# A fused attention and FFN kernel: a third pair of batches in seven products, attention in whole float32

## The chip, the core and the metric

The kernel runs on one core of one Trainium2 chip. The time is device microseconds from the first to the last instruction with what lies around them; a run's number is one execution, and the number of a kernel is the median of its runs. Five engines take part: TensorE (PE in the profile, its weight loads PEld), VectorE (DVE), ScalarE (ACT), GpSimd (POOL) and SyncE (SP), which here issues every DMA. SBUF has 128 partitions; PSUM, into which TensorE writes, has eight banks here used as 512 float32 columns each.

## The reference

Eight batches, twelve heads of 64, 448 positions, width 768, hidden width 3072:

```python
scores = q @ k.T / sqrt(64) - log(448)        # per batch and head
x = sigmoid(scores) @ v                       # 8 x 12 x 448 x 64, laid out as 8 x 448 x 768
h = (x.T @ U) @ V                             # mixing over positions, rank 32
u = x + h.T
out = u + relu(u @ w_ch1) @ w_ch2             # 768 -> 3072 -> 768
```

All arrays are float32. The launch hands U, V and both weight matrices over as 64-bit words (`np.asarray(...)` viewed as int64), and the kernel makes float32 of them itself.

## The kernel before

**Stages.** Attention of a batch goes pair of heads by pair of heads (`pair`, L583): scores of a tile of 128 keys by 448 queries for both heads (`scores_of`, L535, matmuls in L547; the last 64 keys of two neighbouring pairs share a tile, L551), a sigmoid (L664), and values (`values_of`, L557, matmuls in L566 and for the shared tile in L576). Two neighbouring pairs are here called a quad; a batch has three. The result x lies in six tiles `ua` or `ub` of 128 channels by 448 positions. `mix` (batches 0 and 1) or `mix_half` (the others, three tiles at a time, matmuls L848 and L858) adds the mixing over positions; the sum u is written to DRAM (`parked`) for all batches but 0.

**Half precision in parts.** Most matmuls take an fp16 high part and an fp16 rest of each operand and add three products (high by high, high by rest, rest by high). The helper `rest` (L404) makes the rest on VectorE, `scaled` (L401) the high part on GpSimd. `decode` (L874) makes such parts of the weights: 48 pieces of 768 KB are loaded (`w_in`), turned into float32 on VectorE (L404) and ScalarE (L453), bounded (L464), split and kept in DRAM (`kept`). In attention the batches 0 and 1 (`WHOLE = 2`) use whole float32 matmuls; for the batches 2 to 7 q, k and v are scaled and split, and each sigmoid tile is copied to fp16 (L692, ScalarE) and its rest made (L404, VectorE).

**The FFN.** The first `PLAIN = 4` batches go one by one: per batch 24 chains of 18 matmuls into the hidden layer (`ffn_in`, L938) and 36 chains of 12 out of it (`ffn_out`, L958), 864 matmuls. The last four batches go in two pairs by a scheme of seven products in place of eight on 2 x 2 blocks (Strassen's scheme in Winograd's form): `in_quad` and `out_quad`, 12 calls each of 63 matmuls, all in L1146. It needs sums of weight blocks (`quarter_sums`: GpSimd L998 and L1002, then ScalarE L1009 and VectorE L1010, kept as `forms`) and sums of the two batches' u (`far_forms`, `near_forms` for the first pair, `u_forms` for the next).

**What sets the order.** The class `Plan` collects every operation with an engine, a cost, what it reads and writes, the buffers that it wants and a place `pos`. `Plan.order` then builds one program per engine: again and again it takes, where something can start first, the operation with the lowest place. `BOND` keeps TensorE at one kind of attention matmul, `LATE` is the slack that it gives to TensorE's operations after their inputs (0.546 before). The constants at the head (L59 to L74) place the stages against each other: `BEGIN` gives the begin of each batch's FFN, `LATER` the order of the batches 2 to 7 in attention. What this prints is a fixed order for each engine; on the chip an engine waits for its next instruction's inputs and never takes a later one first.

**Homes.** Buffers that are not in use at the same time lie in the same SBUF: the decoding's float32 pieces (`T32`) lie over `stg` (the split q, k, v), over `at` (sigmoids before splitting) and over the second of two `us` (u in fp16 parts for the plain FFN); the mixing's `xs` and `xt` lie in `w64`, in which the weights arrive. `qk` has three homes, `v` four, `a` (sigmoids) seven.

Of the kernel before, what the change touches and what calls it, by code (L numbers as in the profile page):

```python
# [61 lines left out]
ROOM0, ROOM, AHEAD, BEFORE, PACE = -7.852, 308.311, -53.442, 95.466, 1.111  # L62
PREP, BOUNDS, VALUES, SECOND, MIXED = 19.918, -15.21, 0.731, 3.0, 3.524
MIXED1, MIX_1 = 6.837, -10.814
MIX_2, EV_IN, EV_OUT, A_OFF = 34.703, 70.659, 39.745, -7.081
START, DECODE = 63.04, 64.674
U_AT, U_STEP = -3.425, 6.242
LEAD, SUMS, STEP_K, STEP_I, FFN_LEAD = -5.194, 216.012, 10.066, 62.433, 60.97
W_AT, W_STEP, PAIR0, MIX0A, MIX0B, W2_LAG, G0_LEAD = -69.485, 11.668, 3.029, -290.85, -260.87, 0.576, -7.653
LOW_G = 1  # L70
FB, AB = 8, 0
# [23 lines left out]
class Plan:  # L95
# [37 lines left out]
    def order(self):  # L133
# [19 lines left out]
        def room(i):  # L153

            when, taken = 0.0, []
            for t in self.ops[i][7]:
                if t.got is None:
                    if t.in_turn and self.queues[t.name][0] is not t:
                        return None
# [75 lines left out]
def fused_kernel(ctx: ExitStack, tc: tile.TileContext, q, k, v, wu, wv, w1, w2, out):  # L235
# [29 lines left out]
    US = ring("us", 2, [NP, 2, S], F16)  # L265
# [4 lines left out]
    a_, at_ = buf("a", [14 * S], F32), buf("at", [4 * S], F32)  # L270
    A2 = [Buffer(a_[:, 2 * i * S : 2 * (i + 1) * S]) for i in range(7)]
    AT2 = [Buffer(at_[:, 2 * i * S : 2 * (i + 1) * S]) for i in range(2)]
    QK = ring("qk", 3, [2, S], F32)
    V32 = ring("v", 4, [4, P], F32)
# [11 lines left out]
    for x in XT + XS:  # L286
        x.shares += WSRC
        WSRC[0].shares.append(x)
    for x in XT + XS + WS + WSRC:
        x.shares += W64  # L290
        for b in W64:
            b.shares.append(x)
# [55 lines left out]
    for i in range(8):  # L348
        spots(stg[:, 2 * i * S : 2 * (i + 1) * S], under(2 * i * S, 2 * (i + 1) * S))
# [1060 lines left out]
```

## Time and profile before

| What | Value |
|---|---|
| Median of 3 runs | 1537.73 us (1536.45 to 1542.45) |
| The profiled execution | 1541.77 us, of it 1540.0 us from the first to the last instruction |
| Granted TensorE clock, mean | 0.996 |
| Moved by DMA | 306.01 MB |

A page of the profile gives each engine's busy time, a chain of work followed back from the last instruction, and groups of instructions by line. The windows view gives the same busy times for stretches of the span: length, then for PE, PEld, DVE, ACT and POOL the busy us and in brackets the number of instructions, then the granted TensorE clock, the busy share of the DMA engines and GB/s. A row of the chain has start, length and what ran; of the timeline, start, length, engine, line, operation, names and shape. A float32 matmul stands as two records in the chain and in the timeline.

### The profile page before, as it was taken

What the parts mean: (1) busy time and instruction counts of PE and PEld (TensorE: products, weight loads), DVE (VectorE), ACT (ScalarE), POOL (GpSimd) and SP (SyncE); (2) the same over time, 40 slices, a digit from 0 to 9 for tenths busy, and PEclk for the clock granted to TensorE, in tenths of its full rate; (3) what the DMA queues carried; (4) which work ended last, traced back from release to release, by engine and by line L of the source; (5) the groups of instructions that cost most, each with busy time, mean ns of one, the idle gap of its engine ahead of it and who ended that gap; (6) DMA issues with size and microseconds to landing.
All of it is one profiled execution on the core that took longest, in us unless ns stands there. A gap on an engine that the chain in (4) does not pass through costs nothing.

```text
span 1540.0 us, 23899 instructions
## 1 busy us (share of the span) xinstructions
PE 1520.0 (99%) x8843; PEld 752.1 (49%) x8843; DVE 1110.4 (72%) x1864; ACT 814.6 (53%) x1327; POOL 381.9 (25%) x538
## 2 busy tenths in 40 slices
PE   8999899999999999999999999999999999999999
PEld 3344455544444444444444444555555555555554
DVE  2788898668878868766678776776867777565656
ACT  5598766478666666666587735332332614131310
POOL 0110001554234462221322540045454500000000
PEclk9899999999999999999999999999999999999999
DMA  7789876675756858555777656866665673443331
GB/s 215 248 300 272 291 260 253 247 257 162 196 156 171 248 180 208 160 158 167 224 217 205 183 213 173 266 216 229 238 233 180 219 251 113 121 126 108 108 108 72
DMA packets 184725, 306.01 MB, mean 199 GB/s; under 512 B 54560, under 2 KB 146080, under 8 KB 178464
## 3 DMA queue, kind: packets, MB, share of 16 engines
q1 hardware_dynamic: 184608, 304.49, 63.5%
q8 instruction: 69, 1.13, 0.3%
q14 instruction: 48, 0.39, 0.1%
HBM read 232.88 MB, written 63.26 MB: 192 GB/s over the span
## 4 chain that ended last, share of the span: by engine, by line
PE 91%; DMA 4%; DVE 2%; ACT 1%; issue 1%; POOL 0%; SPq 0%; ACTq 0%; POOLq 0%
PE banks L1146 37%; PE banks L958 20%; PE banks L938 19%; PE banks L547 6%; PE banks L566 5%; DMA w<-w_in 2%; PE banks L551 1%; PE banks L576 1%; PE banks L848 1%; DMA qk__99<-q_in 1%; DMA qk__99<-k_in 1%; PE banks L858 0%; DVE stg L404 0%; DMA v__104<-v_in 0%; PE banks L790 0%
## 5 line engine op out<-in xcount | busy, mean ns | idle before, releaser
L958 PE MATMUL banks<-h__94,w__92 128*128 128x448 f16 x792 | 157.9, 353 | 4.3 <-DVE xnt L404 3.2
L958 PE MATMUL banks<-h__93,w__91 128*128 128x448 f16 x792 | 157.8, 353 | 0.7 <-ACT h__94 L946 0.7
L404 DVE SCALAR_TENSOR_TENSOR a<-at,a 128x896 f16<-128x896 f32 (+1 forms) x129 | 141.3, 1118 | 14.9 <-ACT a L692 14.5
L938 PEld LDWEIGHTS <-w__90 128*128 128x128 f16 x936 | 91.1, 98 | 88.7 <-issue 5.4
L958 PEld LDWEIGHTS <-w__92 128*128 128x128 f16 x864 | 82.1, 98 | 88.0 <-issue 15.5
L958 PEld LDWEIGHTS <-w__91 128*128 128x128 f16 x864 | 82.0, 98 | 85.8 <-issue 13.0
L1146 PEld LDWEIGHTS <-w__89 128*128 128x128 f16 x819 | 80.1, 98 | 74.8
L1146 PEld LDWEIGHTS <-w__92 128*128 128x128 f16 x819 | 80.1, 98 | 74.7
L1146 PEld LDWEIGHTS <-w__90 128*128 128x128 f16 x819 | 80.1, 98 | 74.6
L692 ACT ACTIVATE a<-at 128x896 f16<-128x896 f32 x126 | 115.3, 950 | 0.6
L938 PEld LDWEIGHTS <-w__89 128*128 128x128 f16 x792 | 77.0, 98 | 74.1 <-issue 3.5
L1002 POOL TENSOR_TENSOR w<-w 128x384 f32<-128x384 f32 x96 | 105.7, 1101 | 4.8
L938 PE MATMUL banks<-us__87,w__90 128*128 128x448 f16 x504 | 99.1, 352 | 2.3 <-ACT h__94 L946 2.3
L938 PE MATMUL banks<-us__88,w__90 128*128 128x448 f16 x432 | 85.5, 353 | 0.0
L938 PE MATMUL banks<-us__88,w__89 128*128 128x448 f16 x432 | 84.8, 353 | 0.0
L1146 PEld LDWEIGHTS <-w__91 128*128 128x128 f16 x567 | 55.5, 98 | 51.8
L998 POOL TENSOR_TENSOR w<-w 128x384 f32<-128x384 f16 x48 | 44.6, 959 | 117.1 <-DVE xnt L1010 82.0
L547 PE MATMUL banks<-stg 64*128 64x448 f16 x648 | 72.7, 351 | 0.0
L938 PE MATMUL banks<-us__87,w__89 128*128 128x448 f16 x360 | 71.1, 353 | 0.0
L566 PE MATMUL banks<-a,stg 128*64 128x448 f16 x648 | 68.2, 355 | 0.0
L945 ACT ACTIVATE r__95<-banks 128x448 f32<-128x448 f32 x48 | 25.9, 539 | 74.2 <-PE banks L938 73.4
L1009 ACT CAST xnt<-w 128x1536 f16<-128x1536 f32 x24 | 35.2, 1468 | 29.4 <-POOL w L1002 29.4
(1119 smaller groups left out, 3068.4 us busy)
## 6 DMA issues: line engine op xcount, KB each, us to landing
w<-w_in SPq DMA_DIRECT2D x48, 768.0 KB, 6.8
forms<-xnt SPq DMA_DIRECT2D x24, 768.0 KB, 4.4
w__89<-kept SPq DMA_DIRECT2D x9, 1536.0 KB, 7.4
w__90<-kept SPq DMA_DIRECT2D x9, 1536.0 KB, 7.2
w__91<-kept SPq DMA_DIRECT2D x9, 1536.0 KB, 8.5
w__92<-kept SPq DMA_DIRECT2D x9, 1536.0 KB, 7.8
w__90<-forms SPq DMA_DIRECT2D x13, 768.0 KB, 5.4
w__89<-forms SPq DMA_DIRECT2D x13, 768.0 KB, 5.8
```

Source lines behind the costliest of these rows:

```text
L404: nc.vector.scalar_tensor_tensor(out=out, in0=in0, scalar=s, in1=in1, op0=op0, op1=op1)
L547: nc.tensor.matmul(sc[j].x[:, h, :S], x[rows_of(h), j * P : j * P + P], y[rows_of(h)], start=i == 0, stop=i == n - 1)
L551: nc.tensor.matmul(sc[j].x[rows_of(m), h, :S], x[rows_of(h), 3 * P : S], y[rows_of(h)], start=i == 0, stop=i == n - 1)
L566: nc.tensor.matmul(av.x[rows_of(h), :S], x[:, j, rows_of(h)], y(tiles[j], h), start=j == 0 and i == 0, stop=not quad and j == 2 and i == n ...
L692: act(0.95, lambda a=a, to=to: nc.scalar.activation(half(a, 0), to.x, AF.Copy, scale=A_UP), kto, [(a, 0)], here + A_OFF)
L938: nc.tensor.matmul(ph.x[:, :S], w.x[:, f, c, x], us.x[:, c, y, :], start=c == 0 and i == 0, stop=c == NP - 1 and i == 2,)
L945: act(0.54, lambda: nc.scalar.activation(r.x, ph.x[:, :S], AF.Relu, scale=DOWN_H), [ph], [r], pos - EV_IN)
L958: nc.tensor.matmul(po.x[:, :S], w.x[:, f, e, x], h.x[:, f, y, :], start=f == 0 and i == 0, stop=f == FC - 1 and i == 2,)
L998: pool(0.93, lambda j=j: nc.gpsimd.tensor_tensor(out=t.x[:, j], in0=quarter(j, 0), in1=quarter(j, 1), op=ALU.add), [w] if b is None else k ...
L1002: pool(1.0, lambda o_=o_, x=x, y=y, sub=sub: nc.gpsimd.tensor_tensor(out=t.x[:, o_], in0=t.x[:, x], in1=t.x[:, y], op=ALU.subtract if sub ...
L1009: act(1.45, lambda: nc.scalar.copy(made(0), t.x.rearrange(order)), [(t, j) for j in range(4)], [(o, 0)], pos)
L1146: nc.tensor.matmul(bank.x[:, :S], wt[1](k, n, x), both(f)[:, y], start=start and k == i == 0, stop=k == 2 and i == 2, skip_group_check=True)
```

## The change

Six things change together.

1. `PLAIN` goes from 4 to 2: the batches 0 and 1 go one by one, and (2, 3), (4, 5), (6, 7) in seven products. The sums of weight blocks that were spread over three plain batches are all made in batch 1.
2. Attention of all batches is in whole float32 matmuls, as that of 0 and 1 was (`SC32`, `VA32`). The scaling, splitting and bounding of q, k and v, and the splitting of the sigmoids, are not called any more. The sigmoid's output is the value matmuls' input.
3. The value banks are copied out by VectorE (`OUTD`, L751 now) and no longer by ScalarE (L703 before).
4. Homes: `xs` and `xt` get SBUF of their own (`xst`) and no longer share `w64` with the weights; the decoding's pieces lie over `stg` and a new buffer `t32`; `us` has one home in place of two; q and k of batch 0 may also lie in the halves of `h`.
5. A score block, a transpose of the mixing and the first chain into a home of `h` now also wait, in the planner, until the home that their result goes to is free (`"place"`).
6. All constants are new, among them `BOND` (6.183 to 34.831) and `LATE` (0.546 to -2.868: the planner may take an operation of TensorE up to 2.9 us before its inputs are there). Attention of the batches 2 to 7 now begins in the FFN of batch 0.

```diff
 WHOLE = 2
-PLAIN = 4
-LATER = [2, 4, 3, 5, 6, 7]
-FORMS = {1: (0,), 2: (1,), 3: (2,)}
+SC32 = (0, 1, 2, 3, 4, 5, 6, 7)
+VA32 = (0, 1, 2, 3, 4, 5, 6, 7)
+OUTD = (0, 1, 2, 3, 4, 5, 6, 7)
+PLAIN = 2
+LATER = [2, 3, 4, 5, 6, 7]
+FORMS = {1: (0, 1, 2)}
...
-SWITCH, BOND = 0.11, 6.183
-PIPE, LANDS, LATE = 0.33e6, 3.237, 0.546
+SWITCH, BOND = 0.11, 34.831
+PIPE, LANDS, LATE = 0.33e6, 3.237, -2.868
...
-    US = ring("us", 2, [NP, 2, S], F16)
+    US = ring("us", 1, [NP, 2, S], F16)
...
-        n = 1 if b < WHOLE else 3
+        n = 1 if b in SC32 else 3
...
+            if b == 0 or j % 2 == 0:
+                js = (j,) if b == 0 or j and not odd else (j, j + 1)
+                for m in js:
+                    tiles[m] = plan.tile("a2", A2)
+                places = [(tiles[m], "place") for m in js]
...
-            to = a if whole else plan.tile("t2", AT2)
+            to = a if wv else plan.tile("t2", AT2)
...
+            if b in OUTD and wv:
+                dve(0.6, lambda ku=ku, bank=bank: nc.vector.tensor_copy(ku.x, bank.x[:, :S]), [bank], [ku], late)
...
-    XT = [Buffer(w64h[:, : NP * S].rearrange("p (n d) -> p n d", d=P))]
-    XS = [Buffer(w64h[:, NP * S : 2 * NP * S].rearrange("p (c x s) -> p c x s", c=3, x=2))]
+    xst = buf("xst", [2 * NP * S], F16)
+    XT = [Buffer(xst[:, : NP * S].rearrange("p (n d) -> p n d", d=P))]
+    XS = [Buffer(xst[:, NP * S :].rearrange("p (c x s) -> p c x s", c=3, x=2))]
...
-        qk, v32 = plan.tile("qk", QK), plan.tile("v", V32)
+        qk, v32 = plan.tile("qk", QK + QH if b == 0 else QK), plan.tile("v", V32)
...
-            d = (BEGIN[PLAIN] - AHEAD - BEGIN[1]) / (NP * len(LATER) + 0.5)
+            d = (BEGIN[PLAIN] - AHEAD - BEGIN[0] - LATER_AT) / (NP * len(LATER) + 0.5)
             for j, x in enumerate(LATER):
-                attention(x, BEGIN[1] + NP * d * j, d)
+                attention(x, BEGIN[0] + LATER_AT + NP * d * j, d)
```

What this makes of the order is shown at two places. The first is SyncE at the start of the program: `qk` and `v` are homes of q, k and v, `w` the buffer in which weight words arrive, `_in` the inputs in DRAM. Before:

```order
L378 DMA qk__99<-k_in 64x448
L378 DMA qk__99<-q_in 64x448
L378 DMA qk__99<-k_in 64x448
L378 DMA qk__99<-q_in 64x448
L378 DMA v__102<-v_in 128x512
L378 DMA qk__100<-k_in 64x448
L378 DMA qk__100<-q_in 64x448
```

Now:

```order
L408 DMA w_106<-w_in 128x6x128 x2
L408 DMA qk__98<-k_in 64x448
L408 DMA qk__98<-q_in 64x448
L408 DMA qk__98<-k_in 64x448
L408 DMA qk__98<-q_in 64x448
L408 DMA v__101<-v_in 128x512
L408 DMA w_106<-w_in 128x6x128
```

Two weight loads now stand ahead of the first k and q, and a third behind the first v; before, the first three stood together behind the loads of three pairs.

The second is ScalarE in the middle of the attention stage. `a` are sigmoids, `at` sigmoids that are still to be split, `banks` PSUM, `r` and `h` the hidden layer, `ub` the attention's result, `junk` the output that nobody reads of a bound. Before:

```order
L664 ACTIVATE at<-banks,bias_s,c__211 128x896 x2
L692 ACTIVATE a<-at 128x896 x2
L664 ACTIVATE at<-banks,bias_s,c__211 128x896
L464 ACTIVATE junk,ss__194<-v__104 128x512
L692 ACTIVATE a<-at 128x896
L664 ACTIVATE at<-banks,bias_s,c__209 128x896
L464 ACTIVATE junk,ss__194<-qk__100 128x448
L692 ACTIVATE a<-at 128x896
L464 ACTIVATE junk,ss__194<-qk__100 128x448
L664 ACTIVATE at<-banks,bias_s,c__209 128x896
L945 ACTIVATE r__96<-banks 128x448
```

Now:

```order
L705 ACTIVATE a<-banks,bias_s 128x896 x2
L903 ACTIVATE xnt<-banks 128x384
L890 ACTIVATE xst<-ub__84,s_x__194 128x448
L890 ACTIVATE xst<-ub__86,s_x__194 128x448
L996 ACTIVATE r__95<-banks 128x448
L997 ACTIVATE h__94<-banks 128x448
L705 ACTIVATE a<-banks,bias_s 128x896 x5
L996 ACTIVATE r__96<-banks 128x448
L997 ACTIVATE h__94<-banks 128x448
L903 ACTIVATE xnt<-banks 128x384
L705 ACTIVATE a<-banks,bias_s 128x896 x2
```

One or two sigmoids, each followed by its copy, have become runs of up to five sigmoids without anything between, and the copies and bounds are gone.

More of the change, by code (lines that the diff above doesn't have):

```diff
@@ new lines, in fused_kernel, with laid @@
+    for j in range(stg.shape[1] // (2 * PIECE)):
+        lo, hi = j * 2 * PIECE, (j + 1) * 2 * PIECE
+        t = Buffer(stg[:, lo:hi].bitcast(F32))
+        for o in under(lo, hi):
+            t.shares.append(o)
+            o.shares.append(t)
+        T32.append(t)
+    for j in range(T32_N):
+        T32.append(Buffer(t32[:, j * PIECE : (j + 1) * PIECE]))
+        shared.append((j * PIECE, (j + 1) * PIECE, T32[-1]))
+    def laid(lo, n, ap):
+        x = Buffer(ap)
+        for a, b, o in shared:
+            if a < lo + n and lo < b:
+                x.shares.append(o)
+                o.shares.append(x)
+        return lo, lo + n, x
@@ L354, in fused_kernel @@
         spots(x.ap, [x])
+    for i in range(t32.shape[1] // S):
+        spots(t32[:, i * S : (i + 1) * S], [o for lo, hi, o in shared if lo < (i + 1) * S and i * S < hi])
     for i in range(10):
-        spots(w64[:, i * S // 2 : (i + 1) * S // 2], W64 + (WSRC if i < 4 else []) + (XT[:1] if i < 3 else []) + (XS if 3 <= i < 6 else []) + (WS if i >= 6 else []))
+        spots(w64[:, i * S // 2 : (i + 1) * S // 2], W64 + (WSRC if i < 4 else []) + (WS if i >= 6 else []))
+    FORM = SPOT[-4:] + SPOT[-10:-7]
     MID = SPOT[:-10] + SPOT[-6:-4]
+    for i in range(6):
+        spots(xst[:, 2 * i * S : 2 * (i + 1) * S], XT if i < 3 else XS)
+    MID += SPOT[-6:]
     WT = []
@@ L474, in fused_kernel @@
     for b in range(PLAIN):
-        BEGIN.append(BEGIN[-1] + FFN + (ROOM0 if not b else ROOM * len(LATER) / (PLAIN - 1)))
+        BEGIN.append(BEGIN[-1] + FFN + (ROOM0, ROOM)[b])
     def mixing():
@@ L671, in pair @@
             quads[b] = dict(last=[last_products], products=score_products, kscore=kscore, klast=klast)
[L672 to L673 removed]
+            if not ws:
+                quads[b].update(cm=cm)
+            if not wv:
+                quads[b].update(v3=v3)
             quad = None
         products = [quad["products"], score_products] if odd else [score_products]
[L676 removed]
+        sc = {}
         for j in range(3 + odd):
@@ L717, in new_u @@
     def new_u(b):
-        u32s[b] = [plan.tile(f"u{'ab'[b > 0]}{c}", [(UB if b else UA)[c]]) for c in range(NP)]
-        mxs[b] = sm("mx", NP) if b < PLAIN else sm(f"mx{b}", NP, 1)
+        u32s[b] = [plan.tile(f"u{'ab'[b > 0]}{c}", [UB[c]] if b else [UA[c]]) for c in range(NP)]
+        mxs[b] = sm(f"mx{b}", NP, 1)
     def mix(b, pos0, pos1):
@@ L754, in transposes @@
                         )
-                op_ = pe(0.48, transposes, ku[hf * 3 : hf * 3 + 3] + ["ident"] + ([] if whole else [sx]), [tr] + ([tp] if sc == 0 else []), at, after=() if sc == 0 else first)
+                xn = plan.tile("xn", XN)
+                op_ = pe(0.48, transposes, ku[hf * 3 : hf * 3 + 3] + ["ident"] + ([] if whole else [sx]), [tr, (xn, "place")] + ([tp] if sc == 0 else []), at, after=() if sc == 0 else first)
                 first = first if sc else [op_]
-                xn = plan.tile("xn", XN)
                 if whole:
@@ L933, in ffn_in @@
         ph = plan.tile("f", PF[b], False)
+        place = [(h, "place")] if f == 0 else []
         def chain():
@@ L941, in chain @@
                     )
-        entered.append(pe(18 * MM, chain, [(w, 0, f), (w, 1, f)] + [(us, c, x) for c in range(NP) for x in range(2)], [ph], pos, 0.3))
+        entered.append(pe(18 * MM, chain, [(w, 0, f), (w, 1, f)] + [(us, c, x) for c in range(NP) for x in range(2)], [ph] + place, pos, 0.3))
         r = plan.tile("r", R)
```

227 lines of the change are left out of this document (118 added, 109 removed).

## The prediction

> **What bounds the kernel now.** I read the page first, then the busy time by windows, the chain that ended last, the timeline of TensorE, and last the groups of instructions. From the page:
>
> ```profile
> span 1540.0 us, 23899 instructions
> PE 1520.0 (99%) x8843; PEld 752.1 (49%) x8843; DVE 1110.4 (72%) x1864; ACT 814.6 (53%) x1327; POOL 381.9 (25%) x538
> ```
>
> TensorE has 20 us without work; no other engine comes near. A change is worth what it does to TensorE's own work, plus what it does to those 20 us and to stretches where TensorE runs at a lower clock. Where they lie, by windows (columns: length, busy us of PE, PEld, DVE, ACT, POOL, granted clock, DMA share, GB/s):
>
> ```profile
> 0.00:40.00 40.00, 33.45 (x158) 14.36 (x159) 12.43 (x21) 22.48 (x31) 1.21 (x9) 0.96 0.75 212
> 40.00:80.00 40.00, 37.90 (x155) 13.62 (x154) 28.41 (x59) 24.91 (x39) 4.81 (x7) 0.87 0.75 247
> ...
> 160.00:200.00 40.00, 33.47 (x188) 18.42 (x187) 35.75 (x69) 30.97 (x55) 2.33 (x8) 1.00 0.83 293
> 200.00:240.00 40.00, 40.00 (x214) 20.73 (x213) 39.64 (x74) 28.25 (x49) 1.87 (x3) 1.00 0.78 274
> ...
> 480.00:560.00 80.00, 79.59 (x508) 38.38 (x506) 62.08 (x96) 54.54 (x86) 43.55 (x57) 1.00 0.77 222
> ...
> 1500.00:1540.00 40.00, 36.29 (x192) 18.59 (x190) 24.68 (x40) 3.09 (x6) 0.00 (x0) 1.00 0.19 69
> ```
>
> Idle are 6.5 us in 0 to 40, 2.1 in 40 to 80, 6.5 in 160 to 200, 3.7 at the end (the last output's drain), and about 1 in all the rest. In 160 to 240 VectorE is at 35.8 and 39.6 of 40: there it holds TensorE up, with decoding, the mixing of batch 1 and the FFN of batch 0 at once. Between 200 and 1500 TensorE hardly ever waits although VectorE works three quarters of the time.
>
> The lower clock, in 4 us windows:
>
> ```profile
> 24.00:28.00 4.00, 2.13 (x6) 1.83 (x8) 2.48 (x3) 0.71 (x3) 0.00 (x0) 0.74 0.44 122
> 28.00:32.00 4.00, 4.00 (x21) 2.05 (x19) 0.00 (x0) 3.82 (x6) 0.00 (x0) 0.83 0.86 256
> ...
> 64.00:68.00 4.00, 1.91 (x5) 0.63 (x4) 1.87 (x3) 3.57 (x6) 0.00 (x0) 0.86 0.97 328
> 68.00:72.00 4.00, 4.00 (x8) 1.44 (x6) 2.55 (x4) 1.94 (x3) 0.00 (x0) 0.50 0.53 184
> 72.00:76.00 4.00, 4.00 (x14) 1.20 (x16) 3.93 (x8) 2.46 (x3) 0.52 (x1) 0.50 0.59 197
> 76.00:80.00 4.00, 4.00 (x19) 1.48 (x17) 2.33 (x8) 4.00 (x7) 0.74 (x2) 0.86 0.54 145
> ...
> 172.00:176.00 4.00, 1.82 (x10) 0.97 (x10) 3.36 (x5) 3.46 (x7) 0.00 (x0) 1.00 0.63 256
> ```
>
> Loss by it: 4 x (0.26 + 0.17) = 1.7 us near 28, 4 x (0.14 + 0.50 + 0.50 + 0.14) = 5.1 near 70. Idle and slow clock that could go at all: 6.5 - 4.2 (the first load, below) + 2.1 + 6.5 + 1 + 6.8 = 18.7 us.
>
> **The change on TensorE's work.** Block lengths from the chain, for whole float32 (counts are records, two to a matmul), and for chains and products of the FFN:
>
> ```profile
> 4.18 7.82 PE banks L547 x23
> ...
> 25.86 4.46 PE banks L547 x12
> ...
> 80.67 0.91 PE banks L576 x8
> 81.58 0.95 PE banks L547 x4
> ...
> 82.79 1.70 PE banks L547 x8
> 84.49 2.41 PE banks L566 x12
> 86.90 3.51 PE banks L938 x18
> ...
> 91.36 0.91 PE banks L551 x8
> ...
> 126.98 3.40 PE banks L938 x18
> ...
> 1499.97 36.33 PE banks L1146 x192
> ```
>
> and for three half-precision products, from TensorE's timeline (start to the next row's start is the length):
>
> ```profile
> 577.00 1.31 PE L547 MATMUL banks<-stg 64*128 64x448 f16 x12
> 578.24 2.44 PE L958 MATMUL banks<-h__94,w__92 128*128 128x448 f16 x12
> 580.62 1.89 PE L566 MATMUL banks<-a,stg 128*64 128x448 f16 x18
> 582.44 0.76 PE L576 MATMUL banks<-a,stg 64*64 64x448 f16 x12
> 583.13 0.74 PE L547 MATMUL banks<-stg 64*128 64x448 f16 x6
> 583.81 2.44 PE L958 MATMUL banks<-h__94,w__92 128*128 128x448 f16 x12
> ```
>
> Two pairs of heads that share a last tile (I call them a quad; a batch has three) need scores of two tiles and of one, again two and one, the shared score tile, two value blocks and the shared value tile. In float32: 2 x (1.70 + 0.95) + 0.91 + 2 x 2.41 + 0.91 = 11.94 us. In three products: 2 x (1.24 + 0.68) + 0.69 + 2 x 1.82 + 0.69 = 8.86 us, taking the shared score tile like the shared value tile. Before, 6 quads are float32 and 18 are not: 231 us. After, 24 x 11.94 = 286.6. A score block pays once for its start (1.70 is two tiles and 0.95 one, so a tile is 0.75 and the start 0.20; 0.12 in half precision). Counted in the order, the 96 blocks of this sum stand as 84 runs before, 54 after: off go 42 x 0.20 = 8.4 after and about 1.8 before. Attention: 278.2 - 229.2 = **+49.0 us**.
>
> The FFN: a plain pair of batches is 2 x (24 chains of 18 + 36 of 12) = 1728 matmuls, a seven-product pair 24 x 63 = 1512. 216 matmuls less, at 36.33 / 192 = 0.189 us: **-40.9**. A plain chain just ahead of attention takes 0.1 longer (3.51 against 3.40); the order has 66 such places before and 39 after: **-2.7**. Mixing and scaling keep their matmuls. Sum of TensorE's work: **+5.4 us**.
>
> [...]
>
> **The other engines.** For 18 quads these two passes go, 126 of each, and with them the splits of q, k and v and their scales; the copies of the value banks (48) move from ScalarE to VectorE. Rows of the page:
>
> ```profile
> L404 DVE SCALAR_TENSOR_TENSOR a<-at,a 128x896 f16<-128x896 f32 (+1 forms) x129 | 141.3, 1118 | 14.9 <-ACT a L692 14.5
> ...
> L692 ACT ACTIVATE a<-at 128x896 f16<-128x896 f32 x126 | 115.3, 950 | 0.6
> L664 ACT ACTIVATE a<-banks,bias_s 128x896 f32<-128x896 f32 x42 | 40.4, 1007 | 5.5 <-PE banks L547 3.6 <-PE banks L551 1.8
> ...
> L945 ACT ACTIVATE r__95<-banks 128x448 f32<-128x448 f32 x48 | 25.9, 539 | 74.2 <-PE banks L938 73.4 <-DVE h__94 L947 0.8
> ...
> w<-w_in SPq DMA_DIRECT2D x48, 768.0 KB, 6.8
> ```
>
> These 257 us of work ran beside a full TensorE, so taking them away gives nothing by itself. They matter only where TensorE waits.
>
> **The waits, one by one.**
> 1. The first load. SyncE's order now puts two weight loads of 768 KB ahead of the first k and q, whose scores start at 4.18. An issue of such a load takes SyncE 2.06 / 3 = 0.7 us:
>
> ```profile
> 11.64 2.06 SPq L378 DMA_DIRECT2D w<-w_in  x3
> ```
>
> If only the issues count it is 1.4 us; if the two are served first, the second is issued at 1.4 and landed 6.8 later, and q follows after its own 1.4 us of further issues: 9.6, so 5.4. Nothing covers it. Nearer to the second: **+4**.
> 2. The wait near 24 (2.4 idle, 1.7 of clock): three weight loads issued at once stood between the pairs of batch 0 and k and q had three homes. Now the weight loads stand singly and the last three pairs land in the homes of h. Gone: **-4.1**; at the other end it stays, 0.
> 3. 64 to 80 (2.1 idle, 5.1 of clock): mixing of batch 0 in float32 waits for ScalarE and VectorE, both busy with decoding. In the order 11 pairs' value blocks stand ahead of the first FFN chain where 9 stood, so there is more to put between, but mixing and decoding still meet: half, **-3.6**, between 0 and -7.2.
> 4. 160 to 200 (6.5): VectorE full. Between the first and the last output chain of batch 0 there now stand 15 pairs of attention, where 2 stood; at some 6 us a pair TensorE gives the same decoding 78 us more, and decoding and mixing no longer share w64. **-6**, between 0 and -6.5.
> 5. New: runs of scores. The order has 15 runs of five float32 tiles. TensorE needs 5 x 0.75 + 0.20 = 3.95 us, ScalarE's sigmoids 5 x 1.007 = 5.04, and the eight banks hold four tiles. The value block that follows reads its first three tiles first, which gives ScalarE time. **+2**; at worst the difference, 15 x 1.1 = 16.5, and twice that with a pair of relus (2 x 0.54) ahead of each run.
> 6. The later switches (batch 0 to 1, plain to seven products, pair to pair): TensorE hardly waited at any of these before; the single home of us is covered by eight output chains and attention that stand before batch 1's first chain. 0.
>
> Sum: +5.4 + 4 - 4.1 - 3.6 - 6 + 2 = -2.3. Against the profiled execution, 1541.8 (span 1540.0 and 1.8 around it), that is 1539.5. The median of the runs shown, 1537.7, is 4.0 lower; with the same distance the forecast is **1535.5 us**.
>
> On the clock: idle of 1.9 and 2.1 us in a window of 4 near 24 and 64 was followed by 0.74 to 0.50, idle of 2.2 in 172 to 176 by none. [...]
>
> **The rivals.** 0.5% of the time before, 7.7 us, is about what a measurement of this kernel can tell from no change: below 1530.0 is faster, above 1545.4 slower.
> - The forecast: the two bills cancel, and a few waits go. For it: +49.0 and -40.9 come from clean rows. Chance of staying within 0.5%: 0.42.
> - The start is cured (faster): steps 2, 3 and 4 go whole (-4.1 - 7.2 - 6.5 = -17.8), step 1 costs only its issues (+1.4), step 5 nothing: 5.4 + 1.4 - 17.8 = -11.0, 1526.7. For it: every loss lies before 200 us, where VectorE and the loads decide, and both are relieved. Against: all of it must go, and nothing new come, for 11 us. 0.36.
> - ScalarE holds the runs of scores (slower): in place of VectorE's splits, the sigmoids become what the scores wait for, since attention now fills a stretch in which half as many FFN chains stand between. Step 5 at 16.5 to 33: 1550 to 1566. It decides from about 0.8 us a run ((1545.4 - 1533.5) / 15). For it: 1.007 against 0.75 a tile, and runs of five. Against: ScalarE was at 54.5 of 80 with 1.1 + 0.95 a tile. 0.22.
> That the change doesn't do what it says is out: the order holds 4536 seven-product matmuls, three times 1512, and no split of q.
>
> The range, 1519 to 1557: below, the second case less 4 for the scatter of the runs and what else goes in the 18.7; above, the third case to its middle. Faster 0.36, the same 0.42, slower 0.22.
>
> **What would show it.** Right: seven-product work near 858 us (4536 x 0.189), value blocks of 2.41, idle in 160 to 240 gone, first scores at 8 or so. Wrong: first scores at 5.6 and full clock through 100 us speak for the second case; idle of TensorE before runs of scores, ended by ScalarE, and summing to over 12 us, for the third; idle at a switch between pairs would be a cause I have not priced.

## The result: 0.4 to 0.6% slower

| | before | changed |
|---|---|---|
| Median of 8 runs each | 1537.48 us (1533.87 to 1542.45) | 1548.48 us (1545.19 to 1549.18) |
| The profiled execution, its span | 1541.77, 1540.0 us | 1545.25, 1543.5 us |

The ratio is 1.0063, with a 95% interval of 1.0044 to 1.0082; a second measurement (e0) gave 1.0039 (1.0024 to 1.0054). The forecast was 1535.5 us. Its range (1519 to 1557) holds the time; its likeliest case, within 0.5% of the time before, does not hold in the first measurement and just holds in the second.

The page of the changed kernel:

```profile
span 1543.5 us, 21342 instructions
PE 1522.7 (99%) x8050; PEld 736.3 (48%) x8050; DVE 999.6 (65%) x1698; ACT 637.3 (41%) x988; POOL 250.6 (16%) x262
```

TensorE is idle for 20.8 us where it was idle for 20.0, but in other places. The windows (length, busy us of PE, PEld, DVE, ACT, POOL, granted clock, DMA share, GB/s):

```profile
0.00:40.00 40.00, 27.42 (x132) 10.16 (x132) 11.19 (x15) 19.98 (x26) 1.23 (x9) 1.00 0.83 212
40.00:80.00 40.00, 39.63 (x186) 14.79 (x188) 30.83 (x64) 20.45 (x32) 4.11 (x5) 0.96 0.65 217
80.00:120.00 40.00, 38.48 (x211) 15.90 (x204) 32.68 (x63) 30.87 (x45) 3.67 (x5) 1.00 0.84 242
...
160.00:200.00 40.00, 40.00 (x218) 18.11 (x217) 34.35 (x60) 32.85 (x50) 0.00 (x0) 1.00 0.80 284
200.00:320.00 120.00, 118.69 (x634) 53.24 (x633) 99.89 (x181) 89.14 (x133) 9.89 (x11) 1.00 0.91 286
...
24.00:28.00 4.00, 4.00 (x22) 1.48 (x20) 0.00 (x0) 4.00 (x7) 0.00 (x0) 1.00 1.04 277
60.00:64.00 4.00, 4.00 (x12) 1.65 (x11) 4.00 (x7) 0.73 (x2) 0.00 (x0) 0.67 0.01 2
64.00:68.00 4.00, 4.00 (x18) 1.32 (x17) 4.00 (x7) 0.70 (x2) 0.00 (x0) 0.90 0.94 393
```

The idle time of 160 to 200 (6.5 us before) is gone, and so is the wait near 24 with its slow clock; of 64 to 80 there is left a stretch at 0.67 and 0.90. In their place 12.6 us are idle in the first 40, and 1.5 and 1.3 in windows that were full before. The chain that ended last tells the first (start, length, what):

```profile
0.74 0.69 SPq L408
...
2.84 9.61 DMA qk__98<-q_in
12.45 0.14 issue
12.58 5.05 PE banks L577 x12
17.63 2.70 PE banks L596 x12
...
742.33 475.01 PE banks L1197 x2511
1219.17 320.62 PE banks L1197 x1694
```

A q of 112 KB, issued at 2.84 behind two weight loads, landed 9.6 us later; the first score starts at 12.58, not at 4.18. The last two rows are the seven-product stage: 0.189 us a matmul (475.01 / 2511), as before.

**How I add up below.** A kernel's TensorE time is idle time (span less busy), plus what the lower clock takes ((1 - clock) times busy, over all windows of 4 us below 0.985), plus the rest, which I call work. In us:

| | idle 0-40 | 40-120 | 120-200 | later | clock | work |
|---|---|---|---|---|---|---|
| before | 6.6 | 2.1 | 6.5 | 4.8 | 6.1 | 1513.9 |
| before, second profile (f1) | 5.3 | 2.8 | 6.0 | 3.9 | 3.1 | 1515.5 |
| changed | 12.6 | 1.9 | 0 | 6.3 | 1.7 | 1521.0 |
| changed again (e0) | 13.2 | 1.0 | 0 | 6.8 | 1.7 | 1520.7 |

Seven profiles with the old order of TensorE (the kernel before and the experiments below that keep its order) have 1512.5 to 1516.6 of work, eight with the new order 1520.7 to 1525.0, so a single split is good to about 2 us; the means differ by 7.6 us.

### The profile page after: what moved, and what is told of

Its sections match the earlier page's. It is cut to its first block, busy times and chain, and to the rows that moved or that the text cites. A ratio compares the mean times of both kernels' runs of the same rounds, so it can differ in the third digit from the quotient of the medians.

```text
span 1543.5 us, 21342 instructions
## 1 busy us (share of the span) xinstructions
PE 1522.7 (99%) x8050; PEld 736.3 (48%) x8050; DVE 999.6 (65%) x1698; ACT 637.3 (41%) x988; POOL 250.6 (16%) x262
## 4 chain that ended last, share of the span: by engine, by line
PE 96%; DMA 2%; ACT 1%; DVE 0%; issue 0%; SPq 0%
PE banks L1197 56%; PE banks L1009 10%; PE banks L989 10%; PE banks L577 7%; PE banks L596 7%; PE banks L581 1%; PE banks L606 1%; DMA qk__98<-q_in 1%; PE banks L900 1%; DMA w<-w_in 1%; DMA xst<-xst 1%; PE banks L910 0%; PE banks L815 0%; PE banks L803 0%; PE banks L450 0%; PE banks L841 0%
## 5 line engine op out<-in xcount | busy, mean ns | idle before, releaser
L705 ACT ACTIVATE a<-banks,bias_s 128x896 f32<-128x896 f32 x168 | 159.0, 1007 | 88.7 <-PE banks L577 88.6
L1197 PEld LDWEIGHTS <-w__90 128*128 128x128 f16 x1197 | 117.1, 98 | 109.3
L1197 PEld LDWEIGHTS <-w__89 128*128 128x128 f16 x1197 | 117.1, 98 | 109.2
L1197 PEld LDWEIGHTS <-w__92 128*128 128x128 f16 x1134 | 111.0, 98 | 104.1 <-issue 0.8
L1197 PEld LDWEIGHTS <-w__91 128*128 128x128 f16 x1008 | 98.6, 98 | 92.1
L1053 POOL TENSOR_TENSOR w<-w 128x384 f32<-128x384 f32 x96 | 102.6, 1069 | 5.6
L989 PE MATMUL banks<-us__87,w__90 128*128 128x448 f16 x432 | 85.5, 353 | 0.0
L989 PE MATMUL banks<-us__87,w__89 128*128 128x448 f16 x432 | 85.3, 353 | 0.0
L577 PE MATMUL banks<-qk__98 64*128 64x448 f32 x264 | 64.0, 574 | 14.2 <-DMA qk__98<-q_in 14.1
L1009 PEld LDWEIGHTS <-w__91 128*128 128x128 f16 x504 | 48.2, 98 | 52.6 <-issue 9.8
L989 PEld LDWEIGHTS <-w__89 128*128 128x128 f16 x432 | 41.7, 98 | 43.2 <-issue 5.6
L989 PEld LDWEIGHTS <-w__90 128*128 128x128 f16 x432 | 41.8, 98 | 41.7 <-issue 3.8
L1009 PE MATMUL banks<-h__94,w__91 128*128 128x448 f16 x288 | 57.7, 353 | 0.0
L1197 PE MATMUL banks<-a,w__89 128*128 128x448 f16 x249 | 55.4, 352 | 0.0
L1197 PE MATMUL banks<-a,w__90 128*128 128x448 f16 x246 | 55.2, 352 | 0.0
L1197 PE MATMUL banks<-a,w__92 128*128 128x448 f16 x249 | 54.8, 352 | 0.0
L1009 PEld LDWEIGHTS <-w__92 128*128 128x128 f16 x360 | 34.7, 98 | 36.2 <-issue 4.8
L1061 DVE TENSOR_TENSOR xnt<-w,xnt 128x1536 f16<-128x1536 f32 x24 | 42.0, 1751 | 13.3 <-ACT xnt L1060 13.2
L434 DVE SCALAR_TENSOR_TENSOR stg<-w,stg 128x768 int32<-128x768 int32 (+1 forms) x49 | 46.2, 955 | 2.1 <-ACT stg L483 0.9
L434 DVE SCALAR_TENSOR_TENSOR t<-w,t 128x768 int32<-128x768 int32 (+1 forms) x49 | 45.4, 945 | 1.5 <-ACT t L483 1.0
L577 PEld LDWEIGHTS banks<-qk__98 64*128 64x128 f32 x264 | 25.7, 192 | 41.0 <-issue 22.5
```

Of the source, the lines that this page charges most:

```text
L434: nc.vector.scalar_tensor_tensor(out=out, in0=in0, scalar=s, in1=in1, op0=op0, op1=op1)
L577: nc.tensor.matmul(sc[j].x[:, h, :S], x[rows_of(h), j * P : j * P + P], y[rows_of(h)], start=i == 0, stop=i == n - 1)
L705: act(cost, lambda: nc.scalar.activation(out_(), in_(), AF.Sigmoid, bias=bias_s, scale=c if ws else by.x), kin + ["bias"] + ([] if ws else ...
L989: nc.tensor.matmul(ph.x[:, :S], w.x[:, f, c, x], us.x[:, c, y, :], start=c == 0 and i == 0, stop=c == NP - 1 and i == 2,)
L1009: nc.tensor.matmul(po.x[:, :S], w.x[:, f, e, x], h.x[:, f, y, :], start=f == 0 and i == 0, stop=f == FC - 1 and i == 2,)
L1053: pool(1.0, lambda o_=o_, x=x, y=y, sub=sub: nc.gpsimd.tensor_tensor(out=t.x[:, o_], in0=t.x[:, x], in1=t.x[:, y], op=ALU.subtract if sub ...
```

## The experiments

The kernels of one group ran on one chip beside the kernel before; ratios are to it, with 95% intervals. SP's rows are counted from 0, its first load. An edit shifts the line numbers of an experiment by a few lines against the changed kernel's.

### The noise: the changed kernel and the kernel before once more (e0, f1)

No edit in either.

> The changed kernel once more, as it is, for a profile of its usual time and as the measure for the next three. Every theory: 1548 us, 1.006 of before, first scores at about 12.6 us, TensorE's work 5 us more than before. If the profiled execution lies near 1548.5 and not near 1545.2, the difference of some 3 us lies in a lower granted clock in the first 100 us.

> The kernel before, unchanged, as a kernel of its own: ratio 1.000 (0.9985 to 1.0015), and a second profile of it. The first one lay 4 us above its median (1541.8 against 1537.5 us), and the difference of the two profiles (3.5 us) is less than that of the medians (5 to 11 us). If the spread of the kernel before lies in its waits of the first 200 us, the second profile has other waits there and the same work behind 200 us; if it lies in the granted clock of long stretches, the stretches behind 200 us differ.

e0: 1546.57 us, 1.0039 (1.0024 to 1.0054), the idle times of the table. f1: 1540.08 us, 0.9991 (0.9980 to 1.0002). Its page:

```profile
span 1536.6 us, 23899 instructions
PE 1518.6 (99%) x8843; PEld 750.1 (49%) x8843; DVE 1109.3 (72%) x1864; ACT 813.7 (53%) x1327; POOL 382.3 (25%) x538
```

In the first 200 us the second profile of the kernel before has 4 us less of idle time and slow clock than the first (17.2 against 21.3 in the table), behind 200 us 1 us less. So the part at the start varies from run to run.

The first profile, on which the forecast stands, was no unusual run. Over the six groups and f1 the kernel before ran 132 times, with a median of 1541.0 us: 40% of these runs took at least the 1541.77 us of the first profile, 15% no more than the 1538.45 us of f1's. The time goes with the mean granted clock that is on record for each run: the 18 runs at 0.998 or above have a median of 1538.3 us, the 45 at 0.994 or below one of 1542.9. Of the 14 runs of the changed kernel the five at 0.999 or above took 1544.5 to 1546.6 us, the other nine 1546.5 to 1550.6.

### The two halves (e4, e8)

e4 is the kernel before with the attention part alone:

```diff
-        n = 1 if b < WHOLE else 3
+        n = 1
...
-        three, one = (2.22, 0.74) if b < WHOLE else (1.71, 0.57)
-        whole, odd = b < WHOLE, p % 2
+        three, one = 2.22, 0.74
+        whole, odd = True, p % 2
```

> The kernel before with the attention part of the change alone: all attention in whole float32 matmuls, two pairs of batches in the seven-product FFN kept. If the attention term of the sum is right, PE's busy time goes up by 49 us; with the start of the kernel and its waits as they are, the time is 1541.9 + 49 = about 1591 us, ratio 1.032 (1.028 to 1.034 with up to 6 us of waits freed by the conversions that VectorE no longer makes). If what misled the forecast lies in the work (whole float32 dearer than counted, by switches between the two kinds of matmul or by its weight loads), the increase is 55 us or more, ratio 1.036 and up. The other half, the third pair, is then the difference to the changed kernel: minus 41 us by the sum.

1605.04 us, 1.0423 (1.0406 to 1.0440), and from its page:

```profile
PE 1580.8 (99%) x8267; PEld 751.8 (47%) x8267; DVE 881.6 (55%) x1486; ACT 629.6 (39%) x985; POOL 238.7 (15%) x250
```

With 6.5 us for the clock that is 1574.3 of work, 60.4 over the kernel before where the sum had 49.0. The two terms cannot be taken one at a time: by the orders, e4 has 90 runs of float32 score tiles where the changed kernel has 54 (36 x 0.20 = 7.2 us), and its attention stands in 122 pieces with other work between them where the changed kernel's stands in 61. The sum credited the saving of merged runs to the attention; by these counts it comes only with the third pair. The rest of the 11.4 us is not told apart. From e4 to the changed kernel the work falls by 53.3, where the sum had 43.6. Together: +7.1 against +5.4, so the errors cancel.

e8 tries to keep the third pair and to have cheaper scores; its `W_AT` also puts the first q, k and v ahead of the weight loads:

```diff
-SC32 = (0, 1, 2, 3, 4, 5, 6, 7)
+SC32 = (0, 1,)
...
-W_AT, W_STEP, ... = -213.795, 30.418, ...
+W_AT, W_STEP, ... = -150.0, 30.418, ...
```

> A try at a faster kernel: the changed kernel with three pairs, but the scores of the batches from the third on in three half-precision products as in the kernel before (values and attention stay in whole float32), and the first q, k and v loaded ahead of the weights. Eighteen groups of score tiles get cheaper on PE by 4 x 0.75 - 4 x 0.57 less the odd halves, about 1.7 us each by the sum of the prediction, together minus 30 us of PE work; VectorE gets back some 94 us of conversions, in stretches where it is busy for 40 to 60%. If PE sets the time there, the time is 1545 - 30 - 8 + new waits of 5 to 10 = 1512 to 1520, ratio 0.983. If VectorE's conversions stand in the way of the products' additions in the seven-product stage, which PE waits for, the waits take 20 to 40 us and the ratio is 0.995 to 1.01.

1617.21 us, 1.0499 (1.0485 to 1.0513). The waits of TensorE (line, releaser, us in total, times, longest), of which these are the longest:

```profile
PE banks L577 <- POOL stg L431: 9.4, 3, 4.8
PE banks L910 <- DVE xnt L434: 6.8, 5, 2.0
PE banks L450 <- DVE mm_x__184 L918: 6.1, 1, 6.1
PE banks L989 <- ACT us__87 L869: 5.8, 1, 5.8
```

TensorE is idle for 88 us, 63 of them between 120 and 720 us, and the clock takes 23 more. The work did fall, to 1503.1, by 18 of the 30 us that were hoped for. Of the four waits the longest is for GpSimd's split parts (`stg`); the others are for the mixing (`xnt`), the maximum for a scale (`mm_x`) and u in parts (`us`), which now share VectorE and ScalarE with the splits. The edit also makes the planner build another order, so this shows that the kernel as planned with these constants loses more in waits than the cheaper scores give, not that every order would.

### Two constants that place the weight loads (e1, e2, e3)

```diff
-W_AT = -213.795
+W_AT = -150.0        # e1; -185.0 in e2
```

In e3 the kernel before gets W_AT, W_STEP = -213.795, 30.418.

> The changed kernel with the four first weight loads placed 64 us later, so that the first k and q go ahead of all of them. First load theory (the loss against the forecast is the wait for q behind two weight loads): first scores at about 4.2 us and 8 us off the time, 1540 us, 1.002 of before. Rival (the loads are short of bandwidth in the first 90 us, so that what is saved at the start is waited for later, at the next pairs of q and k or at the first weights): first scores at 4.2, but the idle comes back before 100 us, and the time stays within 2 us of 1548. Rival (waits in the attention stage cost the loss): no change, 1548.

> The changed kernel with one weight load ahead of the first k and q in place of two; TensorE's order is the same. First load theory: first scores between 4.2 and 12.6, at about 8 to 9 us, and half of the 8 us off: 1544 us. Bandwidth rival: first scores earlier, time still 1548.

> The kernel before with its first weight loads as early as in the changed one, two of them ahead of the first k and q. First load theory: first scores at about 12 us in place of 4.2 and some 8 us on the time, less the 4 us of the wait near 24 us if that goes: 1541 to 1546 us, 1.003 to 1.005 of before. Bandwidth rival: the time of before, 1537, since the same bytes are waited for either way.

e1: 1547.77 us, 1.0041 (1.0026 to 1.0055). e2: 1544.72, 1.0025 (1.0012 to 1.0038). e3: 1560.17, 1.0124 (1.0111 to 1.0137). In e1 the first score is back at 4.2 us, yet nothing is won; its waits begin with

```profile
PE banks L1197 <- DMA w__91<-forms: 4.4, 1, 4.4
PE banks L577 <- DMA qk__98<-q_in: 4.2, 1, 4.2
```

The 4.4 us stand before 926 us, in the seven-product stage: the constant moves the whole plan. e3's first score is 8 us late as it should be, and two waits of 6.8 and 6.9 us stand in 160 to 200. e1 and e3 don't isolate the loads and decide nothing. e2 keeps TensorE's order, matmul for matmul. Its first score starts at 7.26 us, 5.3 earlier than in the changed kernel, and its median is 1.9 us under that of e0, which ran beside it; the intervals of the two overlap, and 4 us were expected. Its profile, of its longest run (span 1548.6), shows in addition:

```profile
396.00:400.00 4.00, 2.71 (x12) 1.07 (x10) 3.72 (x7) 2.37 (x2) 0.64 (x1) 0.94 0.63 177
400.00:404.00 4.00, 4.00 (x10) 1.20 (x8) 2.35 (x3) 2.01 (x2) 1.56 (x2) 0.50 1.11 234
404.00:408.00 4.00, 4.00 (x17) 1.38 (x14) 0.78 (x3) 0.00 (x0) 2.90 (x4) 0.70 0.95 297
```

Two pauses for q, 1.3 us together, are followed by 8 us at 0.50 and 0.70, which is a loss of 3.2 us. At the same place e0 has the full clock. That such drops make the 3 us between the changed kernel's runs at 1545 and at 1548 to 1550 fits the granted clocks above; where in those runs the clock fell is not on record, so it stays argued.

### Only SyncE's order (e5, e6, e9, e10, e11)

From here on the plan is made as it was, and only the order in which it is written out is altered, for one engine:

```diff
-        for i in self.order():
+        todo = self.order()
+        sp = [i for i in todo if self.ops[i][0] == "SP"]
+        for i in sp[2:7][::-1]:
+            todo.remove(i)
+            todo.insert(0, i)
+        for i in todo:
```

That is e5: the first q, k and v ahead of the two weight loads. e6 does the reverse to the kernel before (its first two weight loads to the head).

> The changed kernel with one thing undone: SP issues the five loads of the first q, k and v ahead of the two weight loads that stood before them; every other engine has the order of the changed kernel, row for row. If the two loads ahead are worth their whole wait (first score at 12.6 us against 4.2 us in the kernel before, 8.4 us), the first score falls to 4.2 to 4.5 us and the time by 7 to 9 us, to 0.9985 (0.997 to 1.000) of the kernel before, and nothing behind it moves. If instead the wait is only put off (the weights come 3 us later, so the decoding and with it the first mixing are late), the first score is early but the idle time between 40 and 120 us grows by 3 to 8 us and the time falls by 0 to 4 us, to 1.002 to 1.004. My 4 us for this step would have given about 1.0015.

> The kernel before with that one thing done: the first two weight loads are moved to the head of SP's order, and every other engine keeps its order. The mirror of the run above. If two weight loads ahead of the first q and k cost their whole wait, the first score goes from 4.2 to 12 to 13 us and the time up by 8 us, ratio 1.0052 (1.004 to 1.007). If the wait near 24 us and those of 64 to 80 us, which the kernel before has anyway, take up part of it (the decoding is done earlier, so PE waits less there), the time goes up by 0 to 4 us, ratio 1.000 to 1.0025; the idle time of PE from 0 to 80 us, 15.1 us in the kernel before, tells the two apart: 23 us by the first, 15 to 19 us by the second.

e5: 1549.46 us, 1.0060 (1.0043 to 1.0077). e6: 1543.28, 1.0017 (1.0005 to 1.0029). The first score moved by 8 us each time (to 4.2 and to 12.0), and the time hardly. e5's TensorE, from the timeline (the brackets: idle before, and what ended it):

```profile
4.17 6.08 PE L582 MATMUL banks<-qk__98 64*128 64x448 f32 x12 [4.17 <-DMA qk__98<-q_in]
10.18 2.83 PE L601 MATMUL banks<-a,v__101 128*64 128x448 f32 x12
18.28 5.52 PE L582 MATMUL banks<-qk__99 64*128 64x448 f32 x12 [5.27 <-DMA qk__99<-q_in]
```

Now the second pair waits behind three weight loads, and the clock of its windows is 0.72 and 0.50:

```profile
16.00:20.00 4.00, 1.72 (x5) 1.17 (x7) 2.48 (x3) 0.68 (x2) 0.00 (x0) 0.72 0.69 162
20.00:24.00 4.00, 4.00 (x15) 1.59 (x15) 0.00 (x0) 2.18 (x3) 0.00 (x0) 0.50 0.80 243
```

In e6 the start costs 8 us and the time only 2.6: the wait near 24 went with it, as in the changed kernel, and TensorE idles for 1.4 us in 40 to 120 (2.1 and 2.8 in the kernel before), but for 8.2 in 120 to 200 (6.5 and 6.0).

So the weight loads were spaced out, one behind each of the first three pairs: e9 in the changed kernel, e10 in the kernel before; e11 is e9 with the three weight loads near 71 us behind the next q and k as well.

```diff
...
+        first = [sp[n] for n in (2, 3, 4, 5, 6, 0, 8, 9, 10, 11, 12, 1, 14, 15, 16, 17, 18, 7)]
+        todo = first + [i for i in todo if i not in first]
...
```

> The changed kernel with only SP's order altered in its first 20 rows: first the q, k and v of one pair of heads (0.7 MB), then one weight load (0.77 MB), then the next pair, and so on; every other engine as in the changed kernel, row for row. The theory now: PE eats a pair in about 9 us and the transfers move some 0.2 MB per us, so what counts at the start is how many bytes stand between one pair and the next, and two or three weight loads in a row cost 7 to 9 us wherever in the first 20 us they stand. By it, one weight load between two pairs is hidden: first score at 4.2 us and no wait over 1.5 us before 25 us, so that PE's idle time from 0 to 40 us falls from 15 us to about 6 us and the time by 8 to 10 us, ratio 0.998 (0.996 to 1.000). The rival, that the bytes of the first 25 us bound the start whatever their order, has the idle time from 0 to 40 us stay above 11 us and the ratio at 1.003 to 1.006.

> The kernel before with the same spacing: one weight load behind each of the first three pairs, where it had all three behind the third and a half; every other engine keeps its order. The waits of the kernel before near 24 us (4.5 us) and of 64 to 80 us (7.6 us) are late weights, by the steps 2 and 3 of the prediction; with the weights 5 to 10 us earlier the idle time of 40 to 80 us falls by 2 to 5 us, and at the start PE may wait 0 to 3 us for the second pair (it takes both pairs' scores first, so it has only 4.5 us of work to hide a weight load). Time 0 to 5 us down, ratio 0.997 to 1.000. If the loss of the start is bytes alone, nothing changes: 1.000.

> As the run above, and in addition the three weight loads that SP issues near 71 us stand behind the first q and k of the next pair in place of ahead of them. The wait of PE for these near 83 us (2.7 us in the changed kernel's profile, 1.8 us in its second) should go: 1.5 to 3 us less than the run above, ratio 0.9965. If the weights of that place are then late for their decoding, ScalarE and VectorE are behind and a wait of the same size shows up between 120 and 220 us: no difference to the run above.

e9: 1549.30 us, 1.0056 (1.0035 to 1.0076). e10: 1541.23, 1.0007 (0.9993 to 1.0022), with 3.5 us idle in 40 to 120, no less than before. e11: 1549.48, 1.0067 (1.0044 to 1.0090). My theory that spacing hides them fell too. In e9 q and k of the second pair were there in time, but TensorE then stood still:

```profile
12.93 2.53 PE L581 MATMUL banks<-qk__99 64*128 64x448 f32 x12
20.93 1.00 PE L585 MATMUL banks<-qk__98 64*64 64x448 f32 x1 [5.47 <-ACT a L709]
```

It waited for a sigmoid of ScalarE (`a`; the recorded expectations call the sigmoids exponentials), and ScalarE's timeline says why:

```profile
13.02 0.84 ACT L498 ACTIVATE w<-stg 128x768 bf16<-128x768 f32 x1 [1.56 <-DVE stg L438]
13.77 0.18 ACT L498 ACTIVATION_READ_ACCUMULATOR w<-stg 128x1 f32 x1
19.04 0.84 ACT L498 ACTIVATE w<-stg 128x768 bf16<-128x768 f32 x1 [5.09 <-DVE stg L438]
19.79 0.19 ACT L498 ACTIVATION_READ_ACCUMULATOR w<-stg 128x1 f32 x1
19.88 3.89 ACT L709 ACTIVATE a<-banks,bias_s 128x896 f32<-128x896 f32 x4
```

The bound of the second piece of weights stands in ScalarE's order ahead of four sigmoids; the scores of the first three were ready by 15.5. It waits for VectorE's decoding, that for the load (VectorE stood 3.48 us for it, to 16.46), and the sigmoids behind it start at 19.88. The same happens in e11 on VectorE, where the first decoding step of a weight load stands ahead of the copies that free TensorE's banks (VectorE, then TensorE):

```profile
79.02 0.56 DVE L439 TENSOR_SCALAR stg<-w 128x768 int32<-128x768 int32 x1 [4.85 <-DMA w<-w_in]
...
81.56 0.60 DVE L759 COPY ub__81<-banks 128x448 f32<-128x448 f32 x1
```

```profile
82.22 3.36 PE L585 MATMUL banks<-qk__98 64*128 64x448 f32 x8 [3.35 <-DVE ub__81 L759]
```

### The weight steps behind the evictions (f2, f3, f4, f5, f6)

f2 is e9, and in addition ScalarE's bound of the second piece is written out behind the four sigmoids. f3 is e11 with that and with the steps near 80 us behind what TensorE waits for.

```diff
...
+        lists = {e: [i for i in todo if self.ops[i][0] == e] for e in ("ACT", "DVE")}
+        for e, what, behind in (("ACT", (4,), 8),):   # f3: also ("DVE", (73, 75, 77), 80), ("ACT", (47,), 51)
+            for n in what:
+                todo.remove(lists[e][n])
+            at = todo.index(lists[e][behind]) + 1
+            todo[at:at] = [lists[e][n] for n in what]
...
```

> As the run with the loads between (e9), and ScalarE's step for the second weight load moved behind the four exponentials that stood behind it; all else the same. In that run PE stood 5.5 us near 15.5 us waiting for an exponential that was queued on ScalarE behind the step of a weight load that had not landed. If this queue is what ate the gain of the earlier first load, the wait goes, the idle time of 0 to 40 us falls from 9.8 to 4 to 6 us, and the time by about 5 us, ratio 1.0005 to 1.003. If the bytes of the start bound it whatever stands where, the wait appears at the next load, and the ratio stays at 1.005.

> As f2, and the same at the second place: the three weight loads near 74 us behind the q and k (as in e11), and the steps for them moved behind what PE waits for, VectorE's three behind the two evictions of values near 82 us and ScalarE's one behind an exponential. The waits of PE near 78 to 87 us (4.4 us in e11) should go too: 4 to 7 us under f2, ratio 0.997 to 0.999, under the kernel before. If the decoding itself is the bound of the first 120 us (ScalarE's and VectorE's steps then late for the seven products' weights), the same time is lost between 90 and 230 us, where the changed kernel lost 5 us, and the ratio stays within 0.002 of f2.

f2: 1544.26 us, 1.0019 (1.0005 to 1.0034). f3: 1545.25, 1.0027 (1.0014 to 1.0040). f2's ScalarE and TensorE at the same place:

```profile
14.27 3.68 ACT L715 ACTIVATE a<-banks,bias_s 128x896 f32<-128x896 f32 x4
19.54 0.84 ACT L504 ACTIVATE w<-stg 128x768 bf16<-128x768 f32 x1 [1.59 <-DVE stg L444]
```

```profile
13.04 2.53 PE L587 MATMUL banks<-qk__99 64*128 64x448 f32 x12
15.49 0.59 PE L591 MATMUL banks<-qk__98 64*64 64x448 f32 x1
...
18.28 3.30 PE L587 MATMUL banks<-qk__100 64*128 64x448 f32 x12 [1.80 <-DMA qk__100<-q_in]
```

The wait of 5.47 us is gone, one of 1.80 for the third pair is left, and the slow clock that followed it is gone as well (the row after it lasts 1.00 us in e9, 0.59 here). One instruction of ScalarE moved takes the ratio from 1.0056 (1.0035 to 1.0076) to 1.0019 (1.0005 to 1.0034): this is what held e9 back, shown (each ratio is to the kernel before of its own group). It is not what the changed kernel itself waits for at its start, which is the load of q. The same queue leaves f2 a wait of 1.28 us at 26, for a sigmoid behind the next bound. At the second place the edit brought nothing: f3 idles for 3.5 us in 40 to 120, f2 for 2.6, and where f2 waits 2.3 us for q at 81, f3 waits 3.1 us for a sigmoid at 85.

f5 and f6 do the like in the kernel before: f5 at 169 us (one step of ScalarE behind two evictions of the mixing, VectorE's two evictions next to each other), f6 at three more places. f4, f6's first form, writes two bounds out behind a later weight load; they put their scratch output into the buffer that this load has filled, so a part of the weights is wrong there, and its time is that of the same instructions with a wait for this load.

```diff
...
+        for e, what, behind in (("ACT", (165,), 167), ("DVE", (220, 216), 217)):
+        # f6: also ("ACT", (184,), 186), ("ACT", (44,), 45), ("ACT", (51,), 53); f4: (43, 44) behind 47 in place of 44 behind 45
...
```

> The mechanism of f2 applied to the kernel before, to see whether it holds there and whether a version comes out that beats both: ScalarE's and VectorE's steps for weights that have not landed yet are moved behind the evictions that PE waits for, at three places: near 169 us (ScalarE's first step of four weight loads behind two evictions of the mixing, VectorE's likewise), near 186 us (one of ScalarE's behind an eviction of h) and at 62 to 73 us (two bounds and one first step behind a copy for the mixing and two exponentials). Nothing else is changed. If these queues are what PE waits for, the waits of 4.1 us (at 171 us), 1.5 us (at 64.9 us) and 1.6 us (at 187.9 us) shrink by 5 to 6 us together, and with shorter pauses the clock lost near 70 us comes back: minus 5 to 7 us, ratio 0.996 (0.995 to 0.997). If the weights are then late for the FFN, the waits come back as waits of PE for w between 180 and 230 us, and the ratio is 0.999 to 1.001.

> The first of the three places of f4 alone (near 169 us: one step of ScalarE behind two evictions, and VectorE's two evictions of the mixing next to each other). By the queue theory PE's wait near 171 us falls from 3.2 to 4.5 us to about 1 us: minus 3 us, ratio 0.998 (0.997 to 0.999). If the bound is the decoding, 1.000.

> The kernel before with f5's edit, and in addition three steps of ScalarE each moved behind the evictions right after it: one bound behind a copy of the mixing (near 63 us), one first step of weights behind two exponentials (near 71 us), one behind the eviction of a hidden tile (near 186 us). The two bounds that f4 moved past the next weight load stay ahead of that load here. By the queue theory each gives back 0.3 to 1 us beyond f5's 2 us: ratio 0.9975 (0.9965 to 0.999). If what is left there is the decoding itself, the ratio is f5's, 0.9987.

f4: 1542.28 us, 1.0004 (0.9993 to 1.0016), with the wait for the load (3.8 us on ScalarE at 69 us) eating what the rest gave. f5: 1539.37, 0.9987 (0.9976 to 0.9999). f6: 1539.36, 0.9985 (0.9973 to 0.9996). f5 in 160 to 200, and its waits there:

```profile
160.00:200.00 40.00, 34.96 (x194) 18.85 (x193) 37.80 (x71) 32.96 (x57) 2.34 (x8) 1.00 0.86 303
```

```profile
PE banks L965 <- DVE e_w__170 L430: 1.7, 1, 1.7
...
PE banks L965 <- DVE xnt L411: 1.1, 2, 0.9
PE banks L427 <- DVE mm_w__167 L875: 1.1, 1, 1.1
```

The wait for `xnt` (3.2 us before, 4.1 in f1) is down to 1.1, as the queue theory has it; but the wait for the scale of the weights (`e_w`) is 1.7 where it was 1.1 (0.4 in f1), and one of 1.1 for their maximum (`mm_w`) is new, as the other has it: the decoding is later. Both are at work, and the net is 1 to 2 us. The three further places of f6 brought nothing beyond f5. f5 and f6 lie under both kernels, under the one before by about 0.14%: their intervals end just below 1, and it is less than what I called tellable for one measurement.

## Why the prediction was wrong

| Step of the prediction | forecast | measured, profile against profile |
|---|---|---|
| TensorE's work | +5.4 | +7.1 (+7.6 by the means of all profiles) |
| 1, the first load | +4 | +8.4 |
| 2, the wait near 24 | -4.1 | -3.6 |
| 3, 64 to 80 | -3.6 | -4.8 |
| 4, 160 to 200 | -6 | -6.5 |
| 5 and new waits | +2 | +3.0 |
| Sum | -2.3 | +3.6 |

The forecast had the changed kernel 2.2 us under the median before (1535.5 against 1537.7), and it is slower. It lies 13 us under the median of the changed kernel: 5.9 us are in the sum, and 7.2 in the step from the profiled run to the median.

- **Step 1 failed, by 4.4 us**, the largest miss in the sum; even its upper value, 5.4, is 3 us short. It took 6.8 us from issue to landing, the median of such loads, for the second of two loads issued one after the other, and let q follow at once. The two together took until 11 us (VectorE's decoding of the second begins at 11.04), q came behind both, and the first score at 12.58.
- **The work** was right in sum by luck: by e4 its two terms are 11.4 and 9.7 us short in size, with opposite signs.
- **Steps 2, 3 and 4** came out within 1.2 us each. Step 2 went whole: counted by busy time, its wait and slow clock were 3.6 us. That the waits of steps 3 and 4 went for the reasons given there, no run isolates. And the steps are not separate terms. e6 shows the same trade in the kernel before: a start 8 us later costs 2.6 us, and the wait near 24 goes with it. e5 and e9 show that taking step 1 back alone gives nothing: in e5 the second pair then waits 5.3 us behind three weight loads, in e9 TensorE waits 5.5 us for ScalarE, whose order was made for weights that come first. With the order of ScalarE altered as well (f2) the ratio is 1.0019; its interval lies below that of the changed kernel's first measurement and overlaps that of e0.
- **Step 5** came out small and for another reason. ScalarE does not hold the runs of scores: in the whole changed kernel the list of TensorE's waits has 0.4 us for its sigmoids. The 3 us are a q that stands behind weight loads near 80 us (1.5), the mixing's transpose by DMA near 220 us (1.3) and small ones.
- **"With the same distance"** failed by 7.2 us: the forecast took off the 4.0 us by which the profiled run before lay above its median, while the changed kernel's lies 3.2 below its own. The 4.0 us were taken from three runs, and these were low, or the chip was a fast one (which chip they ran on is not on record): the 132 later runs have a median of 1541.0, beside which the profiled 1541.77 is no exception. The changed kernel's profile fell on one of its short runs, with a granted clock of 0.999 where six of the eight runs had 0.996 to 0.998. Besides, the waits that steps 2 to 4 counted as gains vary: counted from f1 they are worth some 4 us less.
- **The rival "the start is cured"** lost its ground with step 1, **"ScalarE holds the runs of scores"** with the 0.4 us above.

What stays open: what the changed kernel would give with its whole order made anew around an early first load. f2 moves loads and one instruction of ScalarE and ends 0.2%, 2.9 us, above the kernel before.

## What to carry to other kernels

With two weight loads issued ahead of q the first score starts at 12.58 us, without them (e5) at 4.17, and in e9 a step of ScalarE that waited 5.1 us for weights held up the sigmoids behind it, and TensorE for 5.5. With the loads alone moved the ratio was 1.0060 (e5) and 1.0056 (e9), with ScalarE's step moved as well 1.0019 (f2): where a load is moved, try the order of the steps that wait for it together with it. Price two loads in a row as one (here the second was in use at 11.04 us), not by the median of a single one (6.8). Take the waits of a profile that will be removed from several profiles: between the two of the kernel before, idle time and slow clock of the first 200 us differ by 4.1 us, the work by 1.6. Three runs are too few for the distance between a profiled run and the median. When two large terms are to cancel, count what is shared between them (here the runs of scores) once, in the kernel where both are done.

## What the runs showed of the hardware

- A load of 112 KB issued at 2.84 us behind two of 768 KB landed after 9.6 us. The two, issued by 2.11, were there for VectorE at 5.74 and 11.04. With no weight load ahead of it (e5) TensorE had this q at 4.17. How the transfers share the DMA engines is not shown.
- The first 12 records of scores took 5.05 us in the changed kernel and 6.08 in e5; the next 12 of the kind in the changed kernel took 2.53, half of 5.05. The granted clock of all these windows reads 1.00. The long first records stand at the first matmuls, whether these begin at 4.17 or at 12.58; the reason is not shown.
- Pauses of 5.3 and 5.5 us (e5, e9) were followed by 0.50 in the window from 20 to 24 and 0.93 in the next, two of 1.3 together (e2, near 398) by 0.50 and 0.70, one of 1.8 (f2) by no drop, and the 12.6 at the start by none. But 0.67 also stood at 60 to 64 us of the changed kernel, where TensorE counts as busy throughout and the window before has 0.4 us idle. These 4 us hold 12 records, all of the mixing: matmuls of `128*32` and `32*128`, and transposes. That these are the reason is not shown.
